# An attention and two MLPs on one core: the opening order of the instructions is made anew, and the later attention pairs stand one MLP chunk earlier

## The chip, the core and the metric

The kernel runs on one NeuronCore of a Trainium2 chip. The metric is the time of one execution on the device in microseconds, the median of three runs. One core has five engines with a queue each: TensorE (PE, with its weight loads shown apart as PEld), VectorE (DVE), ScalarE (ACT), GpSimd (POOL) and SyncE (SP), which issues the DMA transfers here. Each engine executes its queue in the order in which the program wrote it, and waits on semaphores for the others.

## What is computed

A gated linear attention over 4 batches, 8 heads, 768 steps and a head size of 48 is followed by two MLPs over its 3072 tokens of width 384, each with 2048 hidden columns.

```
f = 1.0 / (1.0 + np.exp(-f_logit))
for t in range(S):
    state = f[:, :, t, :, None] * state + np.einsum('bhd,bhe->bhde', k[:, :, t], v[:, :, t])
    y[:, :, t] = np.einsum('bhd,bhde->bhe', q[:, :, t], state)
...
h = x @ w_in;  r = np.maximum(h, 0.0);  x = (r * r) @ w_out
...
h = x @ w_in;  g = h * np.tanh(log1p(exp(h)));  out = g @ w_out
```

## The kernel before

**Attention in units.** The attention is cut into 24 units: 12 chunks of 64 time steps, times two pairs of batches; unit `i` is chunk `i // 2`, batch pair `i % 2`. A unit runs through small steps, named for their engine. DVE clips the gate logits (`v_min`), sums along time (`v_scan`), scales queries and keys (`v_q` twice, `v_k`) and masks the scores (`v_mask` twice). ACT computes exponentials and logarithms (`a_exp`, `a_ln`, `a_dq`, `a_dk`). On PE `m_a` multiplies keys by queries, `m_t` transposes the keys, `m_y` forms the output, and `m_u` forms the update of the state, which DVE adds for the unit after the next (`v_s` twice). ACT and DVE read the output of `m_y` into the MLP's input in two parts that together hold full precision (`a_x`, `v_x`); "x read" means these two. Units of the later part are handled as pairs: `quarters_u` (rows `uq`, for the pair before) and `quarters_a` (rows `aq`) stand back to back on PE, and `v_turn` with `a_turn` (eight ACT instructions of line 500 a unit) take the place of the transpose on PE.

**MLP in chunks.** The first MLP runs over 6 blocks of 512 tokens (4 units), times 16 chunks of 128 hidden columns, so 96 chunk steps. `do_l1 i` is nine products of 128x128 by 128x512 into one PSUM buffer (line 330), `act_a` and `act_b` square the positive part and split it into a high part `gh` and a low part `gl` on ACT and DVE, and `do_l2` is nine products into three accumulators `a0`, `a1`, `a2` (line 341), two chunks later. After the sixteenth `do_l2` of a block, the function `evac` copies `a0` and `a2` on ACT and `a1` on DVE (lines 361 and 363). The second MLP has the same shape with a longer activation. The weights arrive as 64-bit numbers; each chunk of the first MLP's weights is loaded by `load_w` and turned into two parts on ACT and DVE (`w_abs`, `w_shift`, `w_top`, `w_low`, `w_hi`, `w_lo`) before its `do_l1`.

**PSUM.** A pool of five buffers (tag `h`) is handed round in program order to `do_l1`, `m_a`, `m_t`, `m_y` and `m_u`, one buffer each, and to `quarters_u` and `quarters_a`, two each. The next user of a buffer waits until the reader of its last content is done. The accumulators lie in buffers of their own; the tile `warm` shares that of `a0`.

**What sets the order.** The order is written by hand in two parts. The string `START` lists the first 419 operations one by one, up to `do_l1 18`; each engine's queue is what falls to it from that list. After `START`, the function `unit` enters each operation of a unit in a table under a chunk step and a priority (`put(step, priority, ...)`), and `run(i)` writes out step `i`, sorted by priority: ACT's `act_a` of the last chunk comes first (5), then the attention's steps, then `do_l1` (100), the attention's products (110 to 111) and `do_l2` of two steps before (120).

**Fillers.** `m_warm n` issues `n` products of a 128-column constant with itself into `warm`; nothing reads them. Each appears as two records in the trace. One call, `m_warm(14)`, stands ahead of `START`, and `START` holds ten more.

Of the kernel before, what the change touches and what calls it, by code (L numbers as in the profile page):

```python
# [36 lines left out]
START = """
m_warm 14; load_j 0; v_min 0; a_exp 0; load_j 1; load_j 2; load_j 3; a_ln 0; v_min 1; a_exp 1; v_scan 0; a_ln 1;
load_f 0; load_f 1; v_min 2; v_scan 1; a_dq 0; v_min 3; a_dk 0; v_k 0; a_exp 2; a_dq 1; v_q 0 1; v_q 0 0; a_dk 1;
load_v 0; load_w 0; a_ln 2; a_exp 3; eye_kn 0; load_v 1; load_f 2; m_t 0; m_warm 2; v_end 1; v_k 1; v_q 1 1; load_v 2;  # L40
v_scan 2; a_ln 3; load_f 3; v_end 0; v_q 1 0; m_a 0; m_warm 5; v_scan 3; v_mask 0 0; w_abs 0; v_mask 0 1; m_a 1;
m_warm 4; a_dq 2; a_dk 2; v_mask 1 1; load_v 3; a_dq 3; v_mask 1 0; m_y 0; a_kn 0; load_w 1; w_shift 0; a_dk 3; v_q 2
0; m_t 1; m_warm 2; w_top 0; eye_kn 1; v_q 2 1; load_w 2; m_y 1; m_warm 3; v_q 3 0; v_k 3; v_k 2; v_q 3 1; w_low 0;
a_x 0; m_u 0; a_kn 1; v_s 0 0; m_a 2; w_abs 1; v_x 0; load_w 3; v_mask 2 0; m_u 1; v_s 1 0; v_s 0 1; w_shift 1; m_a 3;
m_t 3; v_mask 2 1; w_hi 0; a_kn 3; m_t 2; m_warm 1; m_y 2; a_kn 2; v_s 1 1; v_mask 3 1; v_mask 3 0; m_warm 1; m_y 3;
m_warm 1; w_lo 0; w_top 1; load_w 4; w_abs 2; a_x 1; v_x 1; w_shift 2; load_f 5; w_low 1; a_x 2; load_w 5; m_warm 6;
load_w 6; v_end 3; a_x 3; v_x 3; v_x 2; w_top 2; do_l1 0; w_hi 1; w_abs 3; load_v 4; w_lo 1; w_low 2; do_l1 1; w_abs
4; w_shift 3; v_min 5; w_hi 2; load_w 7; w_top 3; a_exp 5; w_lo 2; w_shift 4; m_u 3; load_w 8; w_low 3; act_a 0; act_b
0; w_abs 5; w_top 4; w_hi 3; w_shift 5; load_w 9; do_l1 2; act_a 1; w_lo 3; w_low 4; w_hi 4; act_b 1; load_w 11; w_top
5; w_lo 4; w_low 5; v_s 3 0; do_l2 0; do_l1 3; do_l2 1; act_a 2; act_b 2; do_l1 4; w_abs 6; w_hi 5; w_abs 7; w_shift  # L50
6; w_lo 5; w_top 6; do_l2 2; act_a 3; w_abs 8; w_shift 7; w_low 6; load_f 4; a_ln 5; w_hi 6; w_top 7; act_b 3; v_s 3
1; act_a 4; w_lo 6; w_abs 9; do_l1 5; do_l2 3; w_low 7; w_hi 7; load_v 5; act_b 4; w_shift 8; load_f 7; act_a 5;
w_shift 9; load_w 10; do_l1 6; w_top 8; load_f 6; do_l2 4; v_end 2; w_lo 7; w_top 9; w_low 8; act_b 5; act_a 6; w_hi
8; w_abs 11; v_min 4; v_scan 5; w_lo 8; load_v 7; do_l1 7; w_low 9; load_w 14; a_exp 4; do_l2 5; a_ln 4; act_b 6; a_dq
5; w_hi 9; a_dk 5; v_q 5 1; w_abs 10; w_lo 9; v_scan 4; do_l1 8; act_a 7; do_l2 6; v_k 5; a_dq 4; v_q 5 0; act_a 8;
do_l1 9; a_dk 4; w_shift 10; act_b 7; w_top 10; v_q 4 1; m_t 5; v_min 6; w_shift 11; v_k 4; act_a 9; act_b 8; m_a 5;
load_w 12; do_l2 7; v_min 7; m_u 2; v_q 4 0; do_l2 8; w_low 10; a_kn 5; m_a 4; w_top 11; m_t 4; a_exp 7; v_mask 5 0;
w_hi 10; a_ln 7; w_lo 10; v_end 5; v_end 4; w_low 11; act_b 9; w_abs 12; w_hi 11; w_shift 12; v_mask 5 1; w_top 12;
do_l1 10; do_l2 9; w_lo 11; act_a 10; do_l1 11; w_low 12; load_w 13; w_hi 12; w_abs 13; act_b 10; do_l2 10; v_mask 4
1; w_lo 12; v_s 2 0; v_s 2 1; do_l1 12; act_a 11; w_shift 13; v_mask 4 0; w_abs 14; a_exp 6; act_b 11; m_y 5; a_ln 6;  # L60
w_top 13; w_shift 14; a_kn 4; do_l2 11; w_low 13; v_scan 6; w_hi 13; m_y 4; w_lo 13; act_a 12; do_l1 13; v_scan 7;
w_top 14; a_dq 7; act_b 12; a_dk 7; load_w 15; w_low 14; v_q 7 0; m_u 5; v_s 5 0; v_k 7; a_dq 6; v_q 7 1; do_l2 12;
act_a 13; m_u 4; a_dk 6; m_a 7; act_b 13; v_s 4 0; v_q 6 1; w_hi 14; v_q 6 0; do_l2 13; v_s 5 1; load_v 8; v_k 6; v_s
4 1; v_mask 7 1; m_t 7; a_kn 7; w_abs 15; v_mask 7 0; m_a 6; v_mask 6 1; m_t 6; m_y 7; v_mask 6 0; a_kn 6; load_v 6;
a_x 5; m_y 6; a_x 4; w_lo 14; w_shift 15; do_l1 14; v_end 7; w_top 15; w_low 15; v_x 5; load_f 9; w_hi 15; v_x 4;
load_f 8; v_end 6; m_u 7; act_a 14; w_lo 15; m_u 6; v_s 7 0; v_min 8; v_s 7 1; a_exp 8; v_min 9; do_l1 15; a_ln 8; a_x
6; act_b 14; a_x 7; v_scan 8; v_x 6; a_dq 8; v_x 7; v_s 6 1; do_l2 14; a_dk 8; a_exp 9; v_s 6 0; v_k 8; act_a 15; v_q
8 0; act_b 15; a_ln 9; do_l1 16; v_scan 9; m_t 8; v_end 8; act_a 16; load_v 10; do_l1 17; a_dq 9; v_q 8 1; v_q 9 0;
v_end 9; a_dk 9; load_v 9; do_l2 15; a_kn 8; v_q 9 1; do_l1 18; act_b 16; m_a 8; v_mask 8 1; v_mask 8 0; do_l2 16; m_y
8; m_u 8; act_a 17; load_f 10; act_b 17; v_k 9; v_s 8 0; v_s 8 1  # L70
# [881 lines left out]
```

## Time and profile before

| | |
|---|---|
| median of 3 runs | 889.94 us (889.85 to 890.17) |
| the profiled execution: own time, span | 892.6 us, 890.8 us |
| PE busy | 872.1 us, 98% of the span |
| DVE busy | 683.9 us, 77% |
| ACT busy | 626.6 us, 70% |
| chain that ended last | PE 83%, DVE 9%, DMA 4% |
| mean granted clock of TensorE | 0.993 of full speed |

The busy time of an engine is the time in which at least one of its instructions was running. The ends of PE's products are modelled, and consecutive products overlap (one of 512 columns lasts about 390 ns in the records, while the next starts well before), so a short wait of PE doesn't appear as idle time. The step from the start of one group of products to the start of the next shows it.

### The profile page before, as it was taken

The page shows a single profiled execution, that of the slowest core. Times are in us where ns is not written, and L with a number is a line of the kernel's source. Part 1 is how long each engine was busy: PE and PEld are TensorE (multiplying, and loading weights), DVE is VectorE, ACT ScalarE, POOL GpSimd, SP SyncE. Part 2 cuts the span into 40 slices and gives each one's busy share as a digit, 9 for nine tenths or more (in the row PEclk, how much of TensorE's full clock was granted, in tenths as well). Part 3 has the DMA queues.
Part 4 walks back from the last instruction along what each step waited for, and adds up shares of the span by engine and source line. Part 5 has one row for each costly group of instructions (what it writes and reads, how often), then busy time and mean ns, then how long its engine had stood idle before and what let it go on. Part 6 is the DMA issues. An engine that isn't in the chain of part 4 may idle for free.

```text
span 890.8 us, 16582 instructions
## 1 busy us (share of the span) xinstructions
PE 872.1 (98%) x6619; PEld 720.4 (81%) x6619; DVE 683.9 (77%) x1159; ACT 626.6 (70%) x1151; POOL 6.5 (1%) x21
## 2 busy tenths in 40 slices
PE   8899999999999999999999999999999999999996
PEld 8788778887887888788888888888888888888885
DVE  7899986786988897972122888888888888888875
ACT  7598777987987987954544666676666766676664
POOL 2000000000000000000000000000000000000000
PEclk9799999999999999999999999999999999999999
DMA  9962133535466354632653200200200200200001
GB/s 243 387 199 104 51 124 104 181 128 202 147 198 213 131 202 143 202 107 72 212 181 104 71 1 1 71 1 1 71 0 1 71 1 1 71 1 17 20 0 40
DMA packets 30132, 90.80 MB, mean 102 GB/s; under 512 B 3680, under 2 KB 3680, under 8 KB 30048
## 3 DMA queue, kind: packets, MB, share of 16 engines
q1 hardware_dynamic: 30048, 89.67, 30.0%
q8 instruction: 54, 0.88, 0.4%
q14 instruction: 30, 0.25, 0.1%
HBM read 67.63 MB, written 22.02 MB: 101 GB/s over the span
## 4 chain that ended last, share of the span: by engine, by line
PE 83%; DVE 9%; DMA 4%; ACT 2%; issue 1%; SPq 1%; ACTq 0%
PE a L341 40%; PE h L330 40%; DMA r<-in_w_dram 2%; PE y L545 2%; DVE wbit L255 1%; DMA vs<-in_vv_dram 1%; DVE w L280 1%; DVE gl L354 1%; DVE wbit L258 1%; PE aq L478 1%; PE uq L489 1%; DVE vs L571 1%; DVE mv L520 1%; DVE wbit L252 1%; DVE mv L447 0%
## 5 line engine op out<-in xcount | busy, mean ns | idle before, releaser
L330 PE MATMUL h<-x,w 128*128 128x512 f32 x1728 | 424.8, 390 | 3.9 <-ACT r L721 3.5
L341 PE MATMUL a<-gh,w 128*128 128x512 f32 x1146 | 386.4, 392 | 0.0
L330 PEld LDWEIGHTS h<-x,w 128*128 128x128 f32 x1728 | 323.4, 188 | 72.9 <-ACT r L721 4.8
L341 PEld LDWEIGHTS a<-gh,w 128*128 128x128 f32 x1146 | 215.1, 188 | 45.6
L341 PE MATMUL a<-gl,w 128*128 128x512 f32 x573 | 223.4, 390 | 0.5 <-DVE gl L354 0.5
L788 ACT ACTIVATE e<-e 128x512 f32<-128x512 f32 x95 | 60.0, 632 | 116.1 <-DVE e L787 116.1
L341 PEld LDWEIGHTS a<-gl,w 128*128 128x128 f32 x573 | 107.7, 188 | 23.5 <-DVE gl L354 1.8
L354 DVE TENSOR_TENSOR gl<-r,gh 128x512 fp32r<-128x512 f32 x96 | 65.5, 683 | 74.5 <-ACT gh L349 74.0
L787 DVE TENSOR_SCALAR e<-h 128x512 f32<-128x512 f32 x95 | 65.7, 692 | 59.2 <-PE h L330 56.7
L721 ACT ACTIVATE r<-h 128x512 f32<-128x512 f32 x96 | 56.5, 588 | 52.8 <-PE h L330 52.1
L782 ACT ACTIVATE r<-u,cst 128x512 f32<-128x512 f32 x94 | 67.9, 722 | 8.7 <-DVE u L796 2.7
L796 DVE SCALAR_TENSOR_TENSOR u<-e 128x512 f32<-128x512 f32 x95 | 66.0, 694 | 10.0 <-ACT e L788 0.7
L354 DVE TENSOR_TENSOR gl<-g,gh 128x512 fp32r<-128x512 f32 x95 | 65.8, 693 | 0.0
L784 DVE TENSOR_TENSOR e<-h,u 128x512 f32<-128x512 f32 x94 | 64.4, 685 | 0.0
L791 DVE TENSOR_TENSOR g<-e,r 128x512 f32<-128x512 f32 x94 | 64.2, 683 | 0.0
L722 ACT ACTIVATE r<-r 128x512 f32<-128x512 f32 x96 | 60.7, 633 | 3.1
L349 ACT ACTIVATE gh<-r 128x512 fp32r<-128x512 f32 x96 | 60.7, 633 | 3.1
L349 ACT ACTIVATE gh<-g 128x512 fp32r<-128x512 f32 x95 | 60.1, 633 | 3.1 <-DVE g L815 0.8
L783 ACT ACTIVATE r<-r 128x512 f32<-128x512 f32 x94 | 59.4, 632 | 3.0
L500 ACT ACTIVATE kn<-kt 32x256 f32<-32x256 f32 (+1 forms) x104 | 37.6, 362 | 1.4
L432 DVE TENSOR_TENSOR_SCAN es<-es,cap 112x520 f32<-112x520 f32 x24 | 29.6, 1232 | 0.8 <-ACT es L428 0.8
L447 DVE TENSOR_TENSOR mv<-in,eq 48x512 f32<-48x512 f32 x40 | 27.4, 685 | 1.4 <-ACT eq L437 0.6
...
## 6 DMA issues: line engine op xcount, KB each, us to landing
...
```

Source lines behind the costliest of these rows:

```text
L330: T.matmul(out=ps, lhsT=w[:, k * 128:(k + 1) * 128], rhs=x[:, s, k], start=(i == 0), stop=(i == 8))
L341: T.matmul(out=acc[m], lhsT=w[:, m * 128:(m + 1) * 128], rhs=gx, start=(fc == 0 and i == 0), stop=(fc == FC - 1 and i == 2))
L349: A.activation(out=gh, in_=g, func=AF.Copy)
L354: V.tensor_tensor(out=gl, in0=g, in1=gh.bitcast(F32), op=ALU.subtract)
L722: A.activation(out=r, in_=r, func=AF.Square)
L782: A.activation(out=r, in_=u, func=AF.Ln, bias=two)
L783: A.activation(out=r, in_=r, func=AF.Exp, scale=-1.0)
L784: V.tensor_tensor(out=e, in0=hp, in1=u, op=ALU.mult)
L787: V.tensor_scalar(out=e2, in0=ps, scalar1=20.0, scalar2=None, op0=ALU.min)
L788: A.activation(out=e2, in_=e2, func=AF.Exp)
L791: V.tensor_tensor(out=g, in0=e, in1=r, op=ALU.mult)
L796: V.scalar_tensor_tensor(out=u2, in0=e2, scalar=2.0, in1=e2, op0=ALU.add, op1=ALU.mult)
```

## The change

The change has two parts. In the first, the string `START` is replaced by another order of the same operations. Two operations are added (`a_x 8`, `v_x 8`), which stood in the table before. `a_x` and `v_x` of a unit stand closer behind its `m_y`, the loads come in another order, and the fillers in `START` are 130 calls instead of 39. In the second part, `unit` places the units from 12 on one chunk step earlier, while `m_y` keeps its step; `v_s` of all units from 10 on goes one step earlier too. A new line in the file's `START` moves all later line numbers up by one.

```diff
 START = """
-m_warm 14; load_j 0; v_min 0; a_exp 0; load_j 1; load_j 2; load_j 3; a_ln 0; v_min 1; a_exp 1; v_scan 0; a_ln 1;
...
+m_warm 28; load_j 0; load_f 0; v_min 0; load_j 1; load_j 2; a_exp 0; load_j 3; a_ln 0; load_w 2; eye_kn 0; v_scan 0;
...
             else:
                 odd = i % 2
                 s += 1 - odd
-                end = s + 4
+                end = 8 * (i // 2) - 11
                 if i + 2 < NU:
                     put(s - 1, 27, v_turn, i)
                     put(s + 1 + odd, 14, a_turn, i)
-                    put(s + 9, 12 - odd, v_s, i, 0)
-                    put(s + 10, 9 - odd, v_s, i, 1)
+                    put(8 * (i // 2) - 7, 12 - odd, v_s, i, 0)
+                    put(8 * (i // 2) - 6, 9 - odd, v_s, i, 1)
                 if odd:
                     if i - 2 >= PAIRS:
                         put(s, 110, quarters_u, i - 3, i - 2)
...
             if i >= PAIRS:
-                s = 8 * (i // 2) - 16 + i % 2
+                s = 8 * (i // 2) - (17 if i > PAIRS + 1 else 16) + i % 2
```

**PE's queue ahead of the first MLP product.** In these rows `warm` is a filler, `tr` is `m_t`, `at` is `m_a`, `y` is `m_y` and `u` is `m_u`; the row of `h` is `do_l1 0`. The sixteen rows of each `at` and each `u` are left out. Before:

```order
L592 MATMUL warm<-cap 128x128 x28
L508 MATMUL tr<-idn,in_144 128x112 x4
L592 MATMUL warm<-cap 128x128 x2
...
L592 MATMUL warm<-cap 128x128 x5
...
L592 MATMUL warm<-cap 128x128 x4
L545 MATMUL y<-mv_154,vs_150 32x64 x32
...
L545 MATMUL y<-mv_155,vs_153 32x64 x32
L592 MATMUL warm<-cap 128x128 x7
L330 MATMUL h<-x,w_526 128x512 x9
```

After, the same queue from its start to the same product:

```order
L593 MATMUL warm<-cap 128x128 x42
L509 MATMUL tr<-idn,in_144 128x112 x4
...
L593 MATMUL warm<-cap 128x128 x31
L546 MATMUL y<-mv_154,vs_150 32x64 x32
...
L593 MATMUL warm<-cap 128x128 x10
...
L593 MATMUL warm<-cap 128x128 x23
...
L593 MATMUL warm<-cap 128x128 x15
L546 MATMUL y<-mv_155,vs_153 32x64 x32
L593 MATMUL warm<-cap 128x128 x11
L331 MATMUL h<-x,w_663 128x512 x9
```

The attention's products ahead of `do_l1 0` are the same in both: `m_t`, `m_a` and `m_y` of units 0 to 3, and `m_u` of units 0 and 1. The fillers ahead of it are 53 calls before (the 28, and 2, 5, 4, 2, 3, 1, 1 and 7) and 144 calls after (the 42, and 31, 1, 10, 3, 2, 23, 6, 15 and 11). None stands behind it in either.

**PE's queue where a block of the first MLP ends.** `w_15` is the last chunk of the block, so the rows with `w_15` are `do_l2 31`, after which the accumulators are copied; `w_1` and `w_2` in the rows of `h` are `do_l1 33` and `do_l1 34`. Before:

```order
L330 MATMUL h_2532<-x_1795,w_1_651 128x512 x9
L489 MATMUL uq_2542<-vs2_152,kn0_156 48x48
...
L478 MATMUL aq_2576<-mv1_155,in1_145 64x64
...
L341 MATMUL a2_1724<-gl_2496,w_15_1530 128x512
L341 MATMUL a2_1724<-gh_2487,w_15_1530 128x512
L330 MATMUL h_2667<-x_1795,w_2_673 128x512 x9
```

After, at the same place:

```order
L331 MATMUL h_2592<-x_1858,w_0_663 128x512 x9
L490 MATMUL uq_2602<-vs2_152,kn0_156 48x48
...
L479 MATMUL aq_2636<-mv1_155,in1_145 64x64
...
L342 MATMUL a2_1864<-gl_2549,w_14_1382 128x512
L342 MATMUL a2_1864<-gh_2540,w_14_1382 128x512
L331 MATMUL h_2711<-x_1858,w_1_737 128x512 x9
...
L342 MATMUL a2_1864<-gl_2587,w_15_1637 128x512
L342 MATMUL a2_1864<-gh_2585,w_15_1637 128x512
L331 MATMUL h_2776<-x_1858,w_2_407 128x512 x9
```

The pair's products moved from just ahead of `do_l2 31` to just ahead of `do_l2 30`, so that a `do_l1` now stands between them and the last products of the block.

**ACT's queue at the same place.** `ot` are the copies of the accumulators, the rows from `h` to `gh` are one `act_a`, and `kn<-kt` is `a_turn`. Before:

```order
L721 ACTIVATE r_2520<-h_2501 128x512
L722 ACTIVATE r_2520<-r_2520 128x512
L349 ACTIVATE gh_2523<-r_2520 128x512
L363 ACTIVATE ot_2619<-a0_1722 128x512
L363 ACTIVATE ot_2625<-a2_1724 128x512
L721 ACTIVATE r_2628<-h_2532 128x512
L722 ACTIVATE r_2628<-r_2628 128x512
L349 ACTIVATE gh_2631<-r_2628 128x512
L500 ACTIVATE kn0_156<-kt0_164 32x8x32 x2
```

After:

```order
L722 ACTIVATE r_2679<-h_2592 128x512
L723 ACTIVATE r_2679<-r_2679 128x512
L350 ACTIVATE gh_2682<-r_2679 128x512
L501 ACTIVATE kn0_156<-kt0_164 32x8x32 x2
L501 ACTIVATE kn0_156<-kt0_164 32x8x16 x2
L501 ACTIVATE kn0_156<-kt0_164 32x8x32 x2
L501 ACTIVATE kn0_156<-kt0_164 32x8x16 x2
L364 ACTIVATE ot_2730<-a0_1862 128x512
L364 ACTIVATE ot_2736<-a2_1864 128x512
L722 ACTIVATE r_2739<-h_2711 128x512
```

The eight instructions of `a_turn` moved from behind the copies and the next `act_a` to a place ahead of the copies.

## Rows read from the trace of the kernel before

**Rows 1.** Windows: start:end, length, busy us (instructions) by engine, granted clock, DMA share, GB/s.
```profile
30.00:40.00 10.00, 9.29 (x177) 8.08 (x175) 8.83 (x15) 6.81 (x17) 0.00 (x0) 0.74 1.03 355
100.00:120.00 20.00, 19.13 (x370) 15.22 (x369) 19.26 (x31) 13.45 (x30) 0.00 (x0) 1.00 0.40 125
```

**Rows 2.** Waits of PE over the span: waited for, us in total, times, longest.
```profile
PE h L330 <- ACT r L721: 3.5, 3, 1.2
```

**Rows 3.** Timeline of PE, opening: start us, busy us, engine, line, operation, count, idle before.
```profile
1.78 9.37 PE L592 MATMUL warm<-cap 112*128 112x128 f32 x56 [1.78 <-DVE cst L601]
10.98 0.55 PE L508 MATMUL tr<-idn,in 112*128 112x112 f32 x4
11.37 0.62 PE L592 MATMUL warm<-cap 112*128 112x128 f32 x4
11.92 0.27 PE L466 MATMUL at<-mv,in 48*64 48x64 f32 x1
...
13.00 1.38 PE L592 MATMUL warm<-cap 112*128 112x128 f32 x10
...
16.28 1.16 PE L592 MATMUL warm<-cap 112*128 112x128 f32 x8
17.37 1.10 PE L545 MATMUL y<-mv,vs 112*32 112x64 f32 x64
...
35.63 1.10 PE L545 MATMUL y<-mv,vs 112*32 112x64 f32 x64
36.66 1.83 PE L592 MATMUL warm<-cap 112*128 112x128 f32 x14
38.24 0.48 PE L330 MATMUL h<-x,w 128*128 128x512 f32 x1
39.12 0.50 PE L330 MATMUL h<-x,w 128*128 128x512 f32 x1 [0.39 <-DVE x L585]
...
135.47 0.50 PE L330 MATMUL h<-x,w 128*128 128x512 f32 x1
```

**Rows 4.** Window around one `m_u`, instructions on tile `u` alone.
```profile
134.40:135.60 1.20, 0.93 (x32) 0.80 (x32) 0.01 (x1) 0.00 (x0) 1.00 0.36 149
```

**Rows 5.** Timeline of PE and ACT around the end of `do_l2 31`.
```profile
202.87 0.50 PE L341 MATMUL a<-gh,w 128*128 128x512 f32 x1
...
205.25 0.60 ACT L363 ACTIVATE ot<-a 128x512 f32<-128x512 f32 x1 [0.79 <-PE a L341]
...
205.75 0.59 ACT L721 ACTIVATE r<-h 128x512 f32<-128x512 f32 x1
...
206.39 0.50 PE L330 MATMUL h<-x,w 128*128 128x512 f32 x1 [1.17 <-ACT r L721]
```

**Rows 6.** Timeline of PE: `do_l2 39`, also behind a pair, and `do_l1 42`.
```profile
241.89 0.50 PE L341 MATMUL a<-gh,w 128*128 128x512 f32 x1
...
244.06 0.39 PE L330 MATMUL h<-x,w 128*128 128x512 f32 x1
```

**Rows 7.** Timeline of PE in the second MLP: a `do_l1` and the group behind it.
```profile
870.34 2.20 PE L330 MATMUL h<-x,w 128*128 128x512 f32 x9
872.38 0.39 PE L341 MATMUL a<-gh,w 128*128 128x512 f32 x1
```

**Rows 8.** Timeline of PE: the first two products of `do_l2 34`.
```profile
216.73 0.39 PE L341 MATMUL a<-gh,w 128*128 128x512 f32 x1
217.45 0.50 PE L341 MATMUL a<-gl,w 128*128 128x512 f32 x1 [0.33 <-DVE gl L354]
```

**Rows 9.** Groups by line: out<-in, count, busy us, mean ns, idle before.
```profile
L258 DVE SCALAR_TENSOR_TENSOR wbit<-r,wbit 128x768 uint32<-128x768 uint32 x16 | 15.2, 951 | 0.1
L280 DVE SCALAR_TENSOR_TENSOR w<-wbit,w 128x768 fp32r<-128x768 f32 x16 | 15.2, 947 | 0.4 <-ACT w L275 0.3
L500 ACT ACTIVATE kn<-kt 32x256 f32<-32x256 f32 (+1 forms) x104 | 37.6, 362 | 1.4
```

**Rows 10.** Timeline of DVE where the last `v_x` ahead of `do_l1 0` ends.
```profile
38.05 1.02 DVE L585 TENSOR_TENSOR x<-y,x 128x384 fp32r<-128x384 f32 x2
```

More of the change, by code (lines that the diff above doesn't have):

```diff
@@ L37 @@
 START = """
-m_warm 14; load_j 0; v_min 0; a_exp 0; load_j 1; load_j 2; load_j 3; a_ln 0; v_min 1; a_exp 1; v_scan 0; a_ln 1;
[L39 to L67, printed above, removed]
@@ L68 @@
-8 0; act_b 15; a_ln 9; do_l1 16; v_scan 9; m_t 8; v_end 8; act_a 16; load_v 10; do_l1 17; a_dq 9; v_q 8 1; v_q 9 0;
-v_end 9; a_dk 9; load_v 9; do_l2 15; a_kn 8; v_q 9 1; do_l1 18; act_b 16; m_a 8; v_mask 8 1; v_mask 8 0; do_l2 16; m_y
-8; m_u 8; act_a 17; load_f 10; act_b 17; v_k 9; v_s 8 0; v_s 8 1
+m_warm 28; load_j 0; load_f 0; v_min 0; load_j 1; load_j 2; a_exp 0; load_j 3; a_ln 0; load_w 2; eye_kn 0; v_scan 0;
+v_min 1; a_dq 0; v_min 2; a_exp 1; a_dk 0; a_ln 1; v_q 0 1; v_q 0 0; a_exp 2; v_k 0; v_scan 1; load_f 1; a_ln 2;
@@ new lines @@
+a_dq 1; v_min 3; v_end 0; v_scan 2; m_t 0; m_a 0; a_dk 1; w_abs 2; v_q 1 1; a_exp 3; load_v 0; v_mask 0 1; v_q 1 0;
+load_w 0; load_v 3; w_shift 2; v_mask 0 0; a_kn 0; load_v 1; v_end 1; w_top 2; a_ln 3; v_k 1; m_warm 31; m_y 0;
+w_low 2; m_warm 1; m_a 1; a_dq 2; w_hi 2; v_scan 3; load_f 2; m_u 0; v_q 2 1; m_t 1; a_x 0; v_x 0; a_dk 2; load_v 2;
+v_k 2; load_f 3; load_f 4; v_q 2 0; load_w 1; a_dq 3; w_abs 0; m_warm 10; m_t 2; v_mask 1 0; m_a 2; load_w 4;
+eye_kn 1; a_dk 3; w_shift 0; v_end 2; v_mask 1 1; v_s 0 0; v_s 0 1; v_k 3; m_warm 3; m_y 1; w_lo 2; a_kn 2; a_x 1;
@@ new lines @@
+a_kn 1; v_x 1; v_mask 2 1; load_w 3; w_abs 1; v_min 4; v_q 3 0; load_w 6; a_exp 4; m_warm 2; m_t 3; load_f 6;
+v_mask 2 0; w_top 0; w_shift 1; w_low 0; m_warm 23; m_y 2; m_u 1; v_q 3 1; a_x 2; m_warm 6; m_a 3; v_s 1 0; w_hi 0;
+a_kn 3; w_lo 0; v_mask 3 0; v_s 1 1; load_f 5; w_abs 3; v_mask 3 1; load_w 11; load_w 5; w_abs 4; w_top 1; m_warm 15;
+m_y 3; a_ln 4; load_w 8; v_x 2; w_low 1; a_x 3; w_hi 1; v_x 3; w_shift 4; w_shift 3; v_min 6; load_w 9; w_lo 1;
+w_top 3; w_abs 5; w_top 4; w_low 3; m_warm 11; do_l1 0; act_a 0; m_u 2; w_hi 3; v_min 5; w_low 4; v_s 2 1; do_l1 1;
@@ new lines @@
+act_a 1; load_v 5; act_b 0; w_lo 3; w_abs 6; do_l1 2; do_l2 0; load_w 15; w_shift 5; act_b 1; w_hi 4; a_exp 5;
+w_top 5; do_l1 3; load_w 7; act_a 2; w_lo 4; v_scan 4; w_low 5; act_b 2; do_l2 1; load_w 14; w_abs 7; v_s 2 0; w_hi 5;
+w_shift 7; act_a 3; w_lo 5; w_shift 6; a_ln 5; do_l1 4; w_top 7; w_top 6; act_a 4; a_dq 4; load_f 7; do_l2 2; act_b 3;
+load_w 10; do_l1 5; w_low 6; w_hi 6; do_l2 3; v_end 3; w_abs 8; v_scan 5; load_v 4; a_dq 5; w_lo 6; w_low 7; act_b 4;
+m_u 3; a_dk 5; do_l1 6; v_k 5; m_t 5; a_exp 6; w_shift 8; v_q 5 0; w_hi 7; w_lo 7; act_a 5; v_s 3 0; w_abs 9; w_top 8;
@@ new lines @@
+v_q 5 1; w_shift 9; a_kn 5; do_l2 4; do_l1 7; act_b 5; w_low 8; do_l2 5; a_dk 4; act_a 6; m_a 5; v_s 3 1; w_top 9;
+w_hi 8; v_k 4; w_abs 10; act_b 6; act_a 7; m_t 4; w_low 9; w_lo 8; act_b 7; w_shift 10; v_q 4 1; w_hi 9; w_abs 11;
+a_kn 4; load_v 6; w_top 10; do_l2 6; w_lo 9; do_l1 8; v_q 4 0; w_low 10; load_w 12; do_l2 7; v_min 7; w_shift 11;
+a_ln 6; act_a 8; v_mask 5 0; w_abs 12; v_end 5; v_mask 5 1; do_l1 9; act_b 8; w_hi 10; act_a 9; m_a 4; v_mask 4 0;
+w_top 11; w_lo 10; a_exp 7; w_shift 12; w_low 11; load_w 13; m_y 5; w_hi 11; do_l2 8; act_b 9; w_top 12; w_lo 11;
@@ new lines @@
+w_low 12; w_abs 13; v_mask 4 1; do_l1 10; act_a 10; w_hi 12; act_b 10; do_l2 9; w_shift 13; w_lo 12; a_x 5; w_top 13;
+w_abs 14; a_ln 7; w_abs 15; do_l1 11; m_y 4; v_scan 6; w_low 13; v_end 4; v_x 5; act_a 11; w_shift 14; a_x 4;
+do_l2 10; act_b 11; w_hi 13; w_top 14; a_dq 6; v_x 4; w_lo 13; do_l1 12; w_low 14; act_a 12; w_hi 14; a_dk 6; m_u 4;
+v_scan 7; do_l2 11; act_b 12; w_lo 14; v_k 6; do_l1 13; v_q 6 0; m_u 5; a_dq 7; do_l2 12; act_a 13; a_dk 7; m_t 6;
+v_s 4 1; do_l1 14; a_kn 6; v_q 7 0; act_a 14; v_q 6 1; v_s 4 0; v_q 7 1; v_k 7; load_v 7; load_v 8; act_b 13; v_end 6;
@@ new lines @@
+v_s 5 0; m_a 6; v_s 5 1; m_a 7; v_mask 6 1; do_l2 13; v_mask 7 0; load_f 8; v_mask 6 0; v_mask 7 1; v_end 7; m_t 7;
+m_y 6; w_shift 15; a_kn 7; v_min 8; w_top 15; act_b 14; w_low 15; a_exp 8; a_ln 8; v_scan 8; m_y 7; a_x 7; a_x 6;
+w_hi 15; load_f 9; a_dq 8; m_u 7; a_dk 8; w_lo 15; v_min 9; v_x 6; v_k 8; m_u 6; a_exp 9; v_x 7; v_s 7 1; a_ln 9;
+v_s 7 0; v_end 8; do_l2 14; do_l1 15; act_a 15; v_q 8 1; v_q 8 0; v_s 6 1; act_b 15; m_t 8; v_scan 9; do_l1 16;
+a_kn 8; m_a 8; v_s 6 0; act_a 16; a_dq 9; v_mask 8 0; v_mask 8 1; do_l2 15; v_q 9 1; a_dk 9; do_l1 17; act_b 16;
@@ L71 @@
+m_u 8; v_end 9; act_a 17; m_y 8; v_q 9 0; v_k 9; v_s 8 1; load_v 10; a_x 8; load_v 9; do_l2 16; act_b 17; load_f 10;
+v_x 8; do_l1 18; v_s 8 0
 """
```

## The prediction, on record before the changed kernel was run

> **What bounds the kernel now.** I read the table of stages first: TensorE (PE) is busy 98% of the span, and the chain that ended last lies 83% on PE, so the question in each stage is how much of PE's time is not a product that has to be made. Then I read PE's timeline, group by group. In the second MLP nine products take 2.04 us, from 870.34 to 872.38 [rows 7], that is 0.227 us each, and a group that takes longer has waited or has followed another kind of product.
>
> Two places of lost time bear on the change. The first is the opening: `do_l1 0` starts at 38.24 us, and its second product waits until 39.12 for `v_x`, 0.65 us more than a step of 0.227 [rows 3, 10]. Ahead of it PE runs fillers, waits, and has a granted clock of 0.74 between 30 and 40 us [rows 1]. The second is the end of a block of the first MLP. There `do_l1 34` waits 1.17 us for ACT, and this wait occurs three times, 3.5 us in all [rows 2, 5]. The rows tell why: `uq` and `aq` took four of the five `h` buffers, so `do_l1 34` needs the buffer that `act_a 33` reads; on ACT that stands behind the copy of `a2`, which starts only after the last product of `do_l2 31` (205.25, then line 721 at 205.75, then the product at 206.39). From its first product to `do_l1 34`, `do_l2 31` takes 3.52 us. `do_l2 39`, which also follows a pair but ends no block, takes 2.17 [rows 5, 6].
>
> **The later pairs.** One chunk step earlier, the pair stands before `do_l2` 30, 46 and 62, which end no block. One `do_l1` then stands between the pair and the evacuation, so `do_l1 34` takes the first buffer of `uq`, which DVE has read during the step. The gain is three times 3.52 - 2.17 = 1.35 us, so 4.05. The bounds are 0 (the wait goes elsewhere, a rival below) and that. With DVE's work one step earlier, the single wait of `do_l2 34` for `gl` should go too: its second product starts 0.72 us behind the first instead of 0.23, so 0.49 us [rows 8]; it could stay. What is late next: ACT now has eight instructions of 362 ns, 2.9 us, ahead of the copies [rows 9]. The copy of `a0` is not wanted by PE until `do_l2 32`, one `do_l2`'s remainder and one `do_l1` later (1.36 + 2.04 = 3.4 us), so this has cover. `v_min` to `v_turn`, `load_f` and `load_v` move by the same step; their unit's `aq` moves with them, so their lead over it is unchanged, and `m_y` gets one step more behind the masks. I count them as nothing; with that cover gone a single DVE step would cost its own length.
>
> **The opening.** Here the fillers decide, because PE works through its queue in order. A filler call is two records. Eight records last 1.16 us and fourteen 1.83, so a record costs 0.67 / 6 = 0.1117 us and a call 0.223 us [rows 3]. Change of kind adds 0.02 to 0.20 us a batch (fourteen records from 36.66 to 38.24 are 1.58; eight from 16.28 to 17.37 are 1.09); I take 0.15.
>
> The Trainium skill, page "TensorE: Matmul & The Clock Gate", section "Back-to-back issue gap", gives about 81 ns for a pair of weight load and 128-column product in a stream. By that the 144 calls would cost 11.7 us instead of 32.2; the rows here disagree, with two records a call and 111.7 ns a record, and the rows decide.
>
> Now PE's queue after the change, ahead of `do_l1 0`, with no wait at all:
> - The first batch of 42 calls is 28 records longer than that of before, which ended at 10.98: 10.98 + 28 x 0.1117 = 14.11 us. The slow start is in this already.
> - Four `m_t` of 0.39 us (10.98 to 11.37): 1.56. Four `m_a` of 1.08 (11.92 to 13.00): 4.32. Four `m_y` of 1.03 (35.63 to 36.66): 4.12 [rows 3]. Two `m_u` of 0.93: 1.86 [rows 4].
> - Nine more batches, 102 calls: 204 x 0.1117 + 9 x 0.15 = 24.1.
>
> The sum is 50.1 us. So `do_l1 0` starts at 50.1 instead of 38.24: **+11.8 us**. This is a lower bound, at full clock throughout; waits come on top.
>
> Would PE have stood still there anyway? DVE is what could hold it. Ahead of the last `v_x` of units 0 to 3 DVE has four instructions more than before: `w_top`, `w_low` and `w_lo` of chunk 2, about 0.95 us each [rows 9], and one `v_min`, which works on fewer columns and is at most as long: 2.9 to 3.8 us. Before, that `v_x` ended at 39.07 [rows 10]. So without fillers the products could start near 42.9, and the fillers overshoot by some 7 us. The three DVE steps taken early are not work saved for the end: PE's products behind `do_l1 0` are the same ones.
>
> What the later start gives back: the wait of `do_l1 0` itself, 0.65, since eleven fillers, 2.6 us, stand between the last `m_y` and it, and the reading of x, of which DVE's part is 0.51 [rows 10], fits into them. Between `do_l1 0` and `do_l1 19`, 38.24 to 135.47, stand 36 groups of 2.04, five `m_a`, five `m_y`, seven `m_u` and five `m_t`, 92.4 us by the prices above. Some 13 changes of kind at about 0.2 (2.17 against 2.04 behind a pair, and a little ahead of it) make 2.6, so 2.2 us of the 97.2 are waits, and 1.5 without that of `do_l1 0` [rows 3, 4, 6, 7]. The stages show that DVE runs full there (19.26 of 20 us from 100 to 120, PE 19.13) [rows 1]. In the changed order DVE is about 3 us of work ahead, and PE comes 11.8 us later, so some of these waits go; the order has other neighbours, so others may come. I take half, 0.75 us, with bounds 1.5 and -2.
>
> **Sum.** 11.8 - 0.65 - 0.75 - 4.05 - 0.49 = +5.9 us. The profiled execution had a span of 890.8 us and 892.6 as its own time, 2.7 above the median of the runs; the sum is a difference, so I add it to the median: 889.94 + 5.9 = **895.8 us**, 0.7% slower.
>
> **Rivals.**
> - *The pairs bring their wait along.* `v_s`, `a_turn`, the evacuation and a part of the second weights' conversion now fall into one chunk step, and two `v_s` and two masks into the next. If DVE or ACT is late there by the 1.35 us that was won, nothing is won: 895.8 + 4.05 = 899.9 us. For it speaks that the copies stand behind 2.9 us of `a_turn` on ACT [rows 9]; against it that PE has 3.4 us until it needs them, and that each buffer is read a step before its next user. Chance 0.10.
> - *The opening falls behind.* DVE or ACT runs late on the new order of weight conversions, and PE waits as it did before and 2 us more: the give-back of 0.75 becomes a loss of 2, about 898.6 us. For it speaks that DVE runs full [rows 1]; against it that PE starts nearly 12 us later on the same work. Chance 0.08.
> - *The clock falls in spite of the fillers.* The granted clock of 0.74 between 30 and 40 us shows that PE's waits can bring the slow level of 1.2 GHz into this stretch [rows 1]. At half clock, the batch of 31 calls alone costs 6.9 us more: 902 us. Against it: the fillers leave PE hardly a gap. Chance 0.02.
> - *Fillers cost one pass, and the kernel is faster.* If a call took one record's 0.112 us, the queue would end 16 us earlier, at 34, and DVE's 42.9 would set the start. Then +3.8 (42.9 against 39.07) - 0.75 - 4.05 - 0.49 = -1.5 us: 888.4 us. It decides from a call of 0.18 us down, since the 144 calls, 32.2 us, must lose 5.9 for the kernel to break even. The trace of before speaks against it: the first 28 calls show 56 records, and the rows price them. By the page of the Trainium skill named above, "TensorE: Matmul & The Clock Gate", section "Back-to-back issue gap", a call would be cheaper still, and this rival is what that rule would give here. Chance 0.02.
> - *The later start is hidden*, because something behind the opening (the second weights' reading back, a transfer) bounds the end instead of PE: no change. Against it, PE has no long wait after 220 us except the three named [rows 2]. Chance 0.01.
>
> **How the numbers follow.** My own case has 0.77 and gives 895.8 us; its bounds are all waits gone (11.8 - 0.65 - 1.5 - 4.05 - 0.49 = +5.1, so 895.0) and some left (no gain at `do_l2 34`, waits in the opening as before: +7.1, so 897.0). The range reaches above to the first two rivals, 899.9, and below to 893.5: with 0.02 us for each change of kind behind a batch instead of 0.15 the opening is 1.2 us shorter, and the rest is for changes of kind that I have counted as work. A difference of 0.2% (1.8 us) is about what a measurement of this kernel can tell from none. Faster: 0.02 and a little for what I don't see, 0.03. Same: 0.02. Slower: 0.95.
>
> **What the profile after would show.** `do_l1 0` near 50 us, with the first batch of fillers ending near 14.1, and no idle time of PE worth a microsecond between; a granted clock of 1.00 from 20 to 50 us; DVE waiting more for PE in the first 50 us. The waits of line 330's successor for ACT gone, and the group `do_l2 31` at 2.0 to 2.1 us, `do_l2 30` at 2.17. `do_l1 19` some 10 us later than before, and all later groups some 6 us later from `do_l1 66` on. I am wrong in the main step if `do_l1 0` starts before 45 us, and in the second if the three waits of about 1.2 us reappear at any product between `do_l1 32` and `do_l1 38`.

## The result, and the profile after

The changed kernel takes 899.04 us (median of 4 runs, 898.75 to 899.55) against 890.06 (4 runs, 889.85 to 891.43) for the kernel before: a ratio of 1.0098 [1.0081, 1.0116], 9.0 us slower. I had said 895.8 with a range of 893.5 to 899.9 and a chance of 0.95 for slower. The profiled execution took 898.75, with a span of 897.0 us.

The page of the changed kernel, its first lines, the sum of its chain and the group of the fillers (count, busy us, mean ns, idle before):

```profile
span 897.0 us, 16935 instructions
PE 886.7 (99%) x6801; PEld 735.7 (82%) x6801; DVE 683.8 (76%) x1159; ACT 626.9 (70%) x1151; POOL 6.7 (1%) x21
...
PE 89%; DVE 6%; ACT 2%; issue 1%; DMA 1%; SPq 0%; DVEq 0%; ACTq 0%
...
L593 PE MATMUL warm<-cap 112*128 112x128 f32 x288 | 36.8, 289 | 1.8 <-DVE cst L602 1.8
```

PE is busy for more of a longer span, while DVE's and ACT's busy times are what they were. 288 records of fillers stand there, 36.8 us. So the first place to look at is PE's queue ahead of `do_l1 0`. Timeline of PE in the changed kernel, which answers to [rows 3]:

```profile
1.78 11.81 PE L593 MATMUL warm<-cap 112*128 112x128 f32 x84 [1.78 <-DVE cst L602]
13.42 0.55 PE L509 MATMUL tr<-idn,in 112*128 112x112 f32 x4
...
14.98 7.19 PE L593 MATMUL warm<-cap 112*128 112x128 f32 x62
22.09 1.10 PE L546 MATMUL y<-mv,vs 112*32 112x64 f32 x64
...
46.87 2.72 PE L593 MATMUL warm<-cap 112*128 112x128 f32 x22
49.35 2.29 PE L331 MATMUL h<-x,w 128*128 128x512 f32 x9
```

A bracket behind a row gives the idle time ahead of it and what ended that; a row without one follows without such a wait. So from the first filler to the first product of the MLP, PE works through its queue, and the nine products of `do_l1 0` follow each other without one. The windows of the same stretch (columns as in [rows 1]) say the same, and show who waits instead:

```profile
20.00:30.00 10.00, 10.00 (x212) 9.34 (x211) 7.81 (x13) 6.19 (x14) 0.00 (x0) 1.00 1.01 411
30.00:40.00 10.00, 10.00 (x222) 9.52 (x222) 6.25 (x11) 4.33 (x11) 0.00 (x0) 1.00 1.02 421
```

PE 10.00 of 10 at a granted clock of 1.00, its level of 2.4 GHz; DVE is down to 6.25.

The second part of the change shows in the waits of PE over the whole span (waited for, total us, times, longest). This is all of them that the view names:

```profile
PE warm L593 <- DVE cst L602: 1.8, 1, 1.8
PE a L342 <- DVE gl L355: 1.2, 2, 0.6
```

The three waits for ACT of [rows 2] are gone: `do_l2` 31, 47 and 63 take 2.04 us from their first product to the next group. The second line is new.

**The account.** I followed the starts of three groups through the timelines. The kernel before was profiled a second time for it (below, `before_again`).

| start of | before, as in the rows | before, second profile | after |
|---|---|---|---|
| `do_l1 0` | 38.24 | 35.99 | 49.35 |
| `do_l1 19` | 135.47 | 133.21 | 144.00 |
| from `do_l1 19` to `do_l1 82` | | 293.67 | 291.85 |

Behind `do_l1 82` the products of the two keep their distance, 8.95 us, to the last `do_l1`. Against the second profile the opening is 49.35 - 35.99 = 13.4 us later; 13.4 - 10.8 = 2.6 of it is given back up to `do_l1 19`; and the pairs' stretch is 293.67 - 291.85 = 1.8 shorter. 13.4 - 2.6 - 1.8 = +9.0 us, the difference of the medians. The spans of these two executions differ by 8.5 (897.0 - 888.6), since what stands behind the last products took about 0.45 us less in the changed kernel's; I have not followed that.

### The profile page after: what moved, and what is told of

Read it like the earlier page. It is cut to its first block, busy times and chain, and to the rows that moved or that the text cites. A ratio compares the mean times of both kernels' runs of the same rounds, so it can differ in the third digit from the quotient of the medians.

```text
span 897.0 us, 16935 instructions
## 1 busy us (share of the span) xinstructions
PE 886.7 (99%) x6801; PEld 735.7 (82%) x6801; DVE 683.8 (76%) x1159; ACT 626.9 (70%) x1151; POOL 6.7 (1%) x21
## 4 chain that ended last, share of the span: by engine, by line
PE 89%; DVE 6%; ACT 2%; issue 1%; DMA 1%; SPq 0%; DVEq 0%; ACTq 0%
PE h L331 39%; PE a L342 39%; PE warm L593 4%; PE y L546 2%; PE at L467 1%; DMA in<-in_qkf_dram 1%; DVE gl L355 1%; PE u L556 1%; DVE es L433 1%; DVE mv L448 1%; PE aq L479 1%; DVE wbit L256 1%; PE uq L490 0%; DVE vs L568 0%; DVE wbit L259 0%
## 5 line engine op out<-in xcount | busy, mean ns | idle before, releaser
L593 PE MATMUL warm<-cap 112*128 112x128 f32 x288 | 36.8, 289 | 1.8 <-DVE cst L602 1.8
L593 PEld LDWEIGHTS warm<-cap 112*128 112x128 f32 x288 | 35.1, 202 | 2.3 <-DVE cst L602 1.8
```

The costliest lines, as they stand in the source:

```text
L593: T.matmul(out=warm[:, 0:128], lhsT=sm[:, 0:128], rhs=sm[:, 0:128])
```

## The experiments

The theory, A in the expectations: the loss is the order of PE's queue. Each filler call ahead of `do_l1 0` costs PE about 0.22 us, though the data for that product is there long before; the pairs' move gains a little in spite of it. The rivals, which the expectations give with their letters and numbers, put the loss elsewhere: on the new order of DVE's and ACT's work in the opening, on the clock, or on the pairs' new places. Each ratio is to the kernel before, run beside it.

### The two parts apart

`pairs_only` has the string `START` of before and the new `unit`:

```diff
-                end = s + 4
+                end = 8 * (i // 2) - 11
...
-                    put(s + 9, 12 - odd, v_s, i, 0)
-                    put(s + 10, 9 - odd, v_s, i, 1)
+                    put(8 * (i // 2) - 7, 12 - odd, v_s, i, 0)
+                    put(8 * (i // 2) - 6, 9 - odd, v_s, i, 1)
...
-                s = 8 * (i // 2) - 16 + i % 2
+                s = 8 * (i // 2) - (17 if i > PAIRS + 1 else 16) + i % 2
```

> The opening order of before, with only the later pairs moved one chunk step forward. Theory A (the fillers in the opening are paid in full, and the pairs' move is a gain of its own): the three waits for ACT are gone (4.05 us), and new waits for gl like those in the trace of the changed kernel (about 2 us) remain, so 2 to 2.5 us less than before, about 887.7 us. Rival B (the pairs' move only carries its waits elsewhere): within 0.5 us of before.

Measured: 888.16 us (886.00 to 888.77, 10 runs), 0.9969 [0.9959, 0.998]. `opening_only` is the other half, the new `START` with the `unit` of before:

```diff
-m_warm 14; load_j 0; v_min 0; a_exp 0; load_j 1; load_j 2; load_j 3; a_ln 0; v_min 1; a_exp 1; v_scan 0; a_ln 1;
...
+m_warm 28; load_j 0; load_f 0; v_min 0; load_j 1; load_j 2; a_exp 0; load_j 3; a_ln 0; load_w 2; eye_kn 0; v_scan 0;
```

> The new opening order with its 130 fillers, the later pairs as before. Theory A: do_l1 0 near 49.4 us as in the changed kernel, do_l1 19 near 144.0 against 135.5 in the trace of before, and the three waits for ACT are there again: 2 to 2.5 us more than the changed kernel, about 901.3 us. Rival B: the same as the changed kernel, 899 us.

Measured: 901.05 us (900.61 to 901.45, 4 runs), 1.0124 [1.0108, 1.0139]. `do_l1 0` starts at 49.69, and the three waits for ACT, of 1.35 us by the groups' lengths, are back. Against 890.4 for the kernel before beside them, the opening costs 10.65 and the pairs' move gains 2.2; together +8.4, near the 9.0 of both. So the two parts act nearly one by one: the loss is in the opening, and the pairs' move by itself is a gain.

### What the fillers cost

`before_more` adds 45 calls to the last batch ahead of `do_l1 0` in the kernel before, and leaves everything else in place:

```diff
-m_warm 1; w_lo 0; w_top 1; load_w 4; w_abs 2; a_x 1; v_x 1; w_shift 2; load_f 5; w_low 1; a_x 2; load_w 5; m_warm 6;
+m_warm 1; w_lo 0; w_top 1; load_w 4; w_abs 2; a_x 1; v_x 1; w_shift 2; load_f 5; w_low 1; a_x 2; load_w 5; m_warm 51;
```

> Before, with 45 filler calls more in the one batch right ahead of do_l1 0 (52 instead of 7). Theory A: 45 x 0.223 = 10.1 us on the path, less at most 2.2 us of waits behind it that the later start covers: 7.8 to 10.1 us more than before, 898 to 900 us. Rival D (DVE, full from 40 to 120 us, sets the end of the opening, and fillers run beside it): at most 3 us more, 893 us or less.

Measured: 899.38 us (899.16 to 900.19, 4 runs), 1.0107 [1.0091, 1.0123]. The last batch in its timeline of PE, with `do_l1 0` behind it:

```profile
34.33 12.11 PE L592 MATMUL warm<-cap 112*128 112x128 f32 x104
46.20 1.17 PE L330 MATMUL h<-x,w 128*128 128x512 f32 x4
```

The same place in the second profile of the kernel before:

```profile
34.41 1.83 PE L592 MATMUL warm<-cap 112*128 112x128 f32 x14
35.99 0.48 PE L330 MATMUL h<-x,w 128*128 128x512 f32 x1
```

46.20 - 35.99 = 10.2 us for 45 calls, 0.227 a call. Of these 10.2, 8.9 are still there at `do_l1 19` and 9.0 in the time. The old order with more fillers is as slow as the new order, so it is the calls that cost, and not the clock, which was 1.00 in both. The Trainium skill, page "TensorE: Matmul & The Clock Gate", section "Back-to-back issue gap", gives about 81 ns for a weight load with its 128-column product; an estimate by it is 45 x 0.081 = 3.6 us. The run disagrees: two records a call, 113 ns each.

The other end: `after_bare` takes every `m_warm` out of the new `START` in this way, `before_bare` out of the old one; the call ahead of `START` stays.

```diff
-m_warm 28; load_j 0; load_f 0; v_min 0; load_j 1; load_j 2; a_exp 0; load_j 3; a_ln 0; load_w 2; eye_kn 0; v_scan 0;
+load_j 0; load_f 0; v_min 0; load_j 1; load_j 2; a_exp 0; load_j 3; a_ln 0; load_w 2; eye_kn 0; v_scan 0;
...
```

> The changed kernel without any filler in START (the call of 14 ahead of it stays, 14 calls instead of 144). Theory A: PE waits for DVE instead, do_l1 0 near 43 us by DVE's count, 6 to 7 us sooner than with the fillers; some of that comes back as waits for DVE behind it (up to 2.6 us): 893 to 896 us. Rival C (the fillers are worth their price, since PE falls to 1.2 GHz without them and every product of the opening takes twice as long): do_l1 0 at 48 us or later and 898 us or more. Rival D (DVE sets the end of the opening whatever PE does): 899 us.

Measured: 890.44 us (889.08 to 891.55, 11 runs), 1.0001 [0.9992, 1.001]: 8.6 us less than with the 144 calls. A miss: I had expected 893 to 896, with `do_l1 0` near 43 by DVE's count; it starts at 38.03. The rivals named there, 898 us or more and 899, fall too.

> Before without any filler in START. Theory A: 25 calls less ahead of do_l1 0 save nothing, since PE waits for DVE there, and the clock falls to 1.2 GHz for more of the opening: 1 to 2 us more than before, 891.4 to 892.4 us. Rival E (every call paid): up to 39 x 0.223 = 8.7 us less, 882 to 886 us.

Measured: 892.71 us (890.50 to 895.61, 12 runs), 1.0024 [1.0011, 1.0036], 2.0 us more than the kernel before beside it. That is just at the upper end of what the theory gave; the rival's 8.7 us less did not come. Two stages of `after_bare`, then its timeline of PE from `do_l1 0` on:

```profile
10.00:20.00 10.00, 6.51 (x149) 5.92 (x149) 9.26 (x13) 7.73 (x18) 0.00 (x0) 0.52 1.05 286
...
30.00:40.00 10.00, 7.37 (x186) 6.17 (x179) 9.03 (x15) 6.37 (x13) 0.00 (x0) 0.67 1.02 422
```

```profile
38.03 0.80 PE L330 MATMUL h<-x,w 128*128 128x512 f32 x1 [0.59 <-ACT x L581]
39.51 3.78 PE L330 MATMUL h<-x,w 128*128 128x512 f32 x8 [0.69 <-DVE x L585]
```

Without fillers PE waits, and in those stages its clock is near the lower level, 1.2 GHz, for much of the time (0.52 is almost all of it). It shows in the products: nine took 2.29 us in the changed kernel, eight take 3.78 here. But the waits in brackets are for x, so `do_l1 0` could not have been much earlier in this order. Fillers are worth something, then, but how many?

`after_some` keeps the new order and cuts each batch of it (28, 31, 1, 10, 3, 2, 23, 6, 15, 11) to fit DVE: 66 calls ahead of `do_l1 0` instead of 144, with the 14 ahead of `START`.

```diff
-m_warm 28; load_j 0; load_f 0; v_min 0; load_j 1; load_j 2; a_exp 0; load_j 3; a_ln 0; load_w 2; eye_kn 0; v_scan 0;
+m_warm 14; load_j 0; load_f 0; v_min 0; load_j 1; load_j 2; a_exp 0; load_j 3; a_ln 0; load_w 2; eye_kn 0; v_scan 0;
...
-load_w 0; load_v 3; w_shift 2; v_mask 0 0; a_kn 0; load_v 1; v_end 1; w_top 2; a_ln 3; v_k 1; m_warm 31; m_y 0;
+load_w 0; load_v 3; w_shift 2; v_mask 0 0; a_kn 0; load_v 1; v_end 1; w_top 2; a_ln 3; v_k 1; m_warm 10; m_y 0;
...
```

The batches are then 14, 10, 1, 4, 3, 2, 8, 3, 5 and 2.

> The changed kernel with its ten filler batches in START cut from 28, 31, 1, 10, 3, 2, 23, 6, 15, 11 calls to 14, 10, 1, 4, 3, 2, 8, 3, 5, 2 (66 calls in all with the 14 ahead, against 144 in the changed kernel and 14 in after_bare). Theory A (fillers are paid where they outlast a wait, and hold the clock where they don't): less than after_bare, whose products before do_l1 0 ran at half clock for most of the time, about 888 to 889.5 us. Rival E (clock of no weight, and every filler call paid at 0.223 us): after_bare plus 52 x 0.223 = 11.6 us less what waits hide, 893 us or more.

Measured: 888.41 us (886.83 to 890.08, 6 runs), 0.9974 [0.9962, 0.9987]: 10.6 us less than the changed kernel (11.2 if each is held against the kernel before that ran beside it). Its timeline of PE at `do_l1 0`, then a stage of its windows:

```profile
36.00 0.71 PE L593 MATMUL warm<-cap 112*128 112x128 f32 x4
36.67 0.49 PE L331 MATMUL h<-x,w 128*128 128x512 f32 x1
38.28 2.14 PE L331 MATMUL h<-x,w 128*128 128x512 f32 x8 [1.12 <-DVE x L586]
```

```profile
30.00:40.00 10.00, 8.40 (x172) 6.96 (x161) 9.83 (x16) 6.39 (x13) 0.00 (x0) 1.00 1.02 405
```

The clock is 1.00 from 10 to 50 us with 66 calls in this execution, as with 144; now DVE is the full engine (9.83), and PE waits 1.12 us for its x. The Trainium skill, page "TensorE: Matmul & The Clock Gate", section "Why this matters for your kernels", advises to keep TensorE continuously busy for full throughput. The runs agree, with 1.00 here and 0.52 to 0.84 between 10 and 40 us in `after_bare`, and they give the advice a limit: against this execution the 78 further calls bought no clock, and they cost 10.6 us. The 66 do not hold it every time. `both`, further down, has the same opening, and its profiled execution fell to a clock of 0.83 to 0.92 between 20 and 50 us; that run took 890.26 us, still 8.8 less than the changed kernel.

### The kernel before, profiled again

The time is a median, but the rows that I had read came from one execution of 892.6 us, 2.7 above it. `before_again` is the unchanged kernel.

> The kernel before, unchanged, profiled once more. Theory A (the profile of before that the prediction read fell in an execution whose opening ran at half clock for longer than usual): do_l1 0 between 36.0 and 37.5 us instead of 38.24, span 887 to 889.5 us. Rival H (38.24 us is the kernel's own opening): do_l1 0 at 38.2 us again, span 890.8 us.

Measured: 890.26 us, span 888.6, and `do_l1 0` at 35.99 instead of 38.24. Its windows, beside the 0.74 of [rows 1]:

```profile
30.00:40.00 10.00, 8.77 (x165) 7.29 (x166) 9.72 (x16) 7.96 (x20) 0.00 (x0) 1.00 1.02 367
```

So the profile that the prediction read was an execution that lost clock in the opening, and its `do_l1 0` is 2.25 us later. In `before_again` the clock holds in spite of PE's waits. To see whether a filler in that place steadies it, `before_hold` adds a batch of eight calls:

```diff
-a_x 0; m_u 0; a_kn 1; v_s 0 0; m_a 2; w_abs 1; v_x 0; load_w 3; v_mask 2 0; m_u 1; v_s 1 0; v_s 0 1; w_shift 1; m_a 3;
+a_x 0; m_u 0; m_warm 8; a_kn 1; v_s 0 0; m_a 2; w_abs 1; v_x 0; load_w 3; v_mask 2 0; m_u 1; v_s 1 0; v_s 0 1; w_shift 1; m_a 3;
```

> Before, with one batch of 8 filler calls (1.8 us) more, behind m_u 0, where PE waits 1.9 us for DVE in the trace of before. Theory A (these calls run inside a wait and hold the clock): every run at a mean clock of 0.997 or more, and 0.5 to 1.5 us less than before. Rival E (a filler call is paid wherever it stands): 1 to 1.8 us more than before.

Measured: 892.03 us (891.04 to 894.41, 7 runs), 1.0031 [1.0019, 1.0043]. A miss: I had expected 889 to 890, and every run at a clock of 0.997 or more; five of the seven are below, at 0.994 to 0.996. The profiled execution is the fastest of them (891.04). There `do_l1 0` still starts at 35.98, so the eight calls cost nothing ahead of it, and by `do_l1 19` it is 0.9 us behind `before_again`. One place shows in its timeline of PE:

```profile
111.86 0.32 PE L545 MATMUL y<-mv,vs 128*32 128x64 f32 x7 [1.51 <-issue]
```

In this wait of 1.51 us the engine waits for nothing that the profile shows (more on such waits in the last section). The 1.6 us of the medians fits the size of the rival in the expectation, but not its mechanism, since the calls cost nothing where they stand. Why the other runs lose more than the profiled one is open.

### What became of the pairs' gain

In the stretch of the pairs I had expected 4.5 us and found 1.8. Timeline of the changed kernel at `do_l2 33`, ACT, DVE and PE in order of start:

```profile
216.16 0.63 ACT L350 ACTIVATE gh<-r 128x512 fp32r<-128x512 f32 x1
217.04 0.72 DVE L568 TENSOR_TENSOR vs<-uq,vs 48x192 f32<-48x192 f32 x2
218.37 1.72 DVE L518 TENSOR_TENSOR mv<-aq,cmask 64x256 f32<-64x256 f32 x4
220.12 0.69 DVE L355 TENSOR_TENSOR gl<-r,gh 128x512 fp32r<-128x512 f32 x1
220.87 0.50 PE L342 MATMUL a<-gl,w 128*128 128x512 f32 x1 [0.57 <-DVE gl L355]
```

`gh` is there at 216.8, so `act_b`, which makes `gl` (0.69 us), could run. It runs at 220.12, because `v_s` and four masks of the pair stand ahead of it in DVE's queue. In the changed order they fall into its chunk step. The wait is 0.57 in the bracket, and 0.9 us by the group's length. The same happens at `do_l2 37` behind the scan and scaling of a pair, and smaller, 0.14 to 0.29, at seven more, 3.3 us in all, worked out from the lengths of the groups against 2.04 (2.17 behind a pair). `do_l2 34`, which had waited in [rows 8], loses its wait.

That wait has not gone, though: it has moved one chunk with the work that makes it. DVE's timeline in `before_again` has the same instructions in the same order, ahead of the `gl` of `do_l2 34`:

```profile
211.35 0.72 DVE L567 TENSOR_TENSOR vs<-uq,vs 48x192 f32<-48x192 f32 x2
...
212.67 1.72 DVE L517 TENSOR_TENSOR mv<-aq,cmask 64x256 f32<-64x256 f32 x4
214.42 0.69 DVE L354 TENSOR_TENSOR gl<-r,gh 128x512 fp32r<-128x512 f32 x1
```

There it cost 0.6 us by the group's length, at `do_l2 33` it costs 0.9. So `before_again` has 3 x 1.35 + 0.6 us of waits at these groups and about 0.5 in a few others, 5.2 in all, against 3.3 in the changed kernel; the difference is about the 1.8.

`pairs_actb` puts `act_b` ahead of these steps, from `act_b 20` on (on `pairs_only`):

```diff
-                put(i, 17 if i > last else 32, act_b, i - 1)
+                put(i, 17 if i > last else 9.5 if i > 20 else 32, act_b, i - 1)
```

> The opening of before and the pairs' move, and act_b (which makes gl) entered in the table ahead of the masks, the scans and the scaling of queries and keys (priority 9.5 instead of 32, from chunk step 21 on). Theory A (the new waits are DVE's order: gl stands behind masks or scaling while its input is long there): the waits for gl of do_l2 33 and 37 go, 1.4 us, and most of the small ones, so 1.5 to 2.3 us less than pairs_only, about 886.2 us. Rival F (DVE is simply overfull in these steps): act_b early makes masks or scaling late, and the time stays within 0.5 us of pairs_only, 888.2 us.

Measured: 902.36 us (901.64 to 903.42, 4 runs), 1.0131 [1.0116, 1.0146], the worst miss: I had expected some 886, and the rival there was wrong as well. Its waits of PE:

```profile
PE aq L478 <- DVE in L451: 3.2, 5, 0.9
PE h L330 <- ACT r L721: 2.3, 2, 1.7
...
PE aq L478 <- ACT r L721: 1.9, 2, 1.0
...
PE y L545 <- DVE mv L517: 1.7, 2, 1.6
```

The one line for `gl` that is left is 0.2 us at 117.3, ahead of the steps that the edit changes. But `gl` needs `gh` of the same step from ACT, and with `act_b` early DVE stands still until `gh` is there, step after step, while what feeds the pairs (`in`, `mv`) and ACT queues up behind it. The waits of DVE from 130 to 440 us show it, first in `pairs_only`, then here:

```profile
DVE gl L354 <- ACT gh L349: 37.1, 17, 4.2
```

```profile
DVE gl L354 <- ACT gh L349: 65.9, 33, 5.2
```

The lines of PE shown are 9.1 us of the 14.2 that this kernel takes more than `pairs_only`; the rest I have not followed. The lines of PE left out between them are waits of a kind that the kernel before has too (last section).

`pairs_three` moves only the three pairs that stood at the end of a block, and leaves `v_s` at its old step for those units whose `uq` stands with a pair that does not move:

```diff
-                    put(8 * (i // 2) - 7, 12 - odd, v_s, i, 0)
-                    put(8 * (i // 2) - 6, 9 - odd, v_s, i, 1)
+                    late_s = i // 2 % 2 == 0
+                    put(8 * (i // 2) - 7 + late_s, 12 - odd, v_s, i, 0)
+                    put(8 * (i // 2) - 6 + late_s, 9 - odd, v_s, i, 1)
...
-                s = 8 * (i // 2) - (17 if i > PAIRS + 1 else 16) + i % 2
+                s = 8 * (i // 2) - (17 if i // 2 in (6, 8, 10) else 16) + i % 2
```

> The opening of before, and only the pairs of units 12, 16 and 20 one step forward, those whose place had been ahead of a block's last products; v_s follows. Theory A: the three waits go (4.05 us), and of the new waits for gl only those of the moved pairs remain (0.7 us at do_l2 33 and little else; the 0.75 us at do_l2 37 belongs to the pair of unit 14): 3 to 3.5 us less than before, about 887 us. Rival G: load_f of units 16 and 20 now lands only one step and a half ahead of v_min, which holds up DVE: 888 us or more.

Measured: 887.63 us (886.01 to 889.72, 9 runs), 0.9967 [0.9956, 0.9978]. By the lengths of the groups the waits for `gl` between `do_l1 19` and `do_l1 82` fall from 2.9 us in `pairs_only` to 2.0, and that stretch from 291.5 to 290.7; in the medians the two can't be told apart. The median is at the near end of what the theory gave (3.0 us less than before), and the waits that remain are more than the 0.7 that it counted: 0.7 at `do_l2 61` stands beside the 0.9 at `do_l2 33`.

`both` joins `after_some`'s fillers, `pairs_three` and the early `act_b` for one chunk alone:

```diff
-                put(i, 17 if i > last else 32, act_b, i - 1)
+                put(i, 17 if i > last else 9.5 if i == 34 else 32, act_b, i - 1)
```

> The opening of after_some, the three pairs of pairs_three, and act_b ahead of the masks in chunk step 34 alone. Theory A (the parts add): after_some's opening is about 1 us sooner at do_l1 19 than before's with a fast clock, and the wait for gl of do_l2 33 (0.75 us) goes: 886 to 887.5 us. Rival F (DVE is overfull at step 34, and gl early makes something else late there): 888 us or more.

Measured: 887.35 us (885.70 to 890.26, 5 runs), 0.9961 [0.9947, 0.9975]. It beats both kernels and is the lowest median here, but can't be told from `after_some` or `pairs_three`. Its timeline shows that DVE's order was the cause of the wait at `do_l2 33`: with `gl` ahead of the four masks,

```profile
211.64 0.68 DVE L355 TENSOR_TENSOR gl<-r,gh 128x512 fp32r<-128x512 f32 x1
212.35 1.73 DVE L518 TENSOR_TENSOR mv<-aq,cmask 64x256 f32<-64x256 f32 x4
```

the group takes 2.04 us instead of the 2.94 of `pairs_three`, and its second product follows the first at once:

```profile
213.26 0.39 PE L342 MATMUL a<-gh,w 128*128 128x512 f32 x1
213.49 0.39 PE L342 MATMUL a<-gl,w 128*128 128x512 f32 x1
```

About 0.3 us of it comes back at `do_l2 34`, and the stretch from `do_l1 19` to `do_l1 82` is 289.8 us, the shortest here. `after_some` holds the pairs' move too and is no faster than `pairs_only` (888.16), so the new opening, fitted with fillers or not, shows no gain of its own. The profile of `both` is that of its slowest run (last section).

## Why the prediction was right, and where its sizes were off

**The main step was right.** `do_l1 0` was to start near 50.1 and starts at 49.35, with no wait behind the first filler. From the end of the first batch on, the prices were to give 36.0 us, and the trace has 35.9, at a granted clock of 1.00. `before_more` and `after_some` show the reason: calls alone, in the old order, cost the same, and calls taken out of the new order give it back. The rivals on the opening fall: nothing was late but PE's own queue, the clock held, and a call costs two records. The new order by itself shows no worth either way: without fillers the changed kernel takes 890.44 and the old one 892.71, and the 2.3 between them is about what the pairs' move gains by itself, 2.2.

**The start that I subtracted was too late.** "`do_l1 0` starts at 50.1 instead of 38.24: +11.8" was taken from an execution at a lost clock. In `before_again` it is 35.99, and the term becomes 13.4. The difference is 2.25 us. I had noted that the profiled execution was 2.7 us above the median, and added a difference to the median as though the 2.7 stood in both kernels. They stood in the opening (2.25 of them, by the second profile), where the changed kernel's execution lost no clock.

**The first batch** was to end at 14.11 and ends at 13.42: the 28 further records seem to take 11.81 - 9.37 = 2.44 us, not 28 x 0.1117 = 3.13. The price was not wrong: behind the first record, the records' starts are about 213 ns apart at first and 112 later, although the granted clock reads 1.00 throughout. In the profile of before 26 steps are slow, in the changed kernel's 19; seven slow steps fewer are the 0.7 us, nearly all of 50.1 - 49.35. The second profile of before has 29 and `before_hold` 15, so this belongs to the execution and not to the change.

**DVE's part.** "Without fillers the products could start near 42.9" was too late: 38.03 in `after_bare`, 36.67 in `after_some`, with the second product at 38.28. I had put all the new DVE steps behind the old end of `v_x`, 39.07, as if DVE had had no idle time before it; but it was busy for 7.9 and 8.8 us of the two stages from 20 to 40 us. And 39.07 came from the same execution: in `before_again` that `v_x` ends at 36.84. So the fillers overshoot by some 12 us, not 7.

**The give-back** up to `do_l1 19` was mis-sized: 0.65 + 0.75 = 1.4 expected, 2.6 measured. From `do_l1 0` to `do_l1 19` the changed kernel takes 94.65 us, less than the 95.0 that I had counted as work alone, so some of what I took for changes of kind was waiting. `before_more` gives back only 10.2 - 8.9 = 1.3 for a like delay in the old order, so about half seems to come from the new order.

**The pairs.** The mechanism was right: the waits for ACT go, at all three places, and return in `opening_only`. "`v_min` to `v_turn`, `load_f` and `load_v` move by the same step ... I count them as nothing" was the mis-sized term: 4.05 + 0.49 = 4.5 us expected, 1.8 found in the traces and 2.2 in the times. The moved DVE steps did not delay the copies on ACT, which I had weighed, but `gl`, which I had not: it is made by the same engine, in the same step, behind them. The 0.49 at `do_l2 34` did not go either, it moved to `do_l2 33`. That is half of my rival "the pairs bring their wait along": it named DVE beside ACT, but what I weighed for it was ACT's copies.

The parts together: +1.6 on the opening (13.4 - 11.8), of which 2.25 is the start of before and -0.75 the end of the queue; -1.2 on the give-back; +2.7 on the pairs. 5.9 + 1.6 - 1.2 + 2.7 = 9.0. Two of these misses partly cancel the others, and 899.04 lies outside the bounds of my own case, 895.0 to 897.0. The range holds it only because it reached up to the two first rivals, and neither of them came as described.
